# A new order of all work in a block-causal attention with a gated linear unit

## The chip, the core and the metric

The kernel runs on one core of a Trainium2 chip, in one launch. The core has a matrix engine (TensorE, in the profile PE, its weight loads PEld), a vector engine (VectorE, DVE), a scalar engine (ScalarE, ACT), a general engine (GpSimd, POOL) and an engine that here only issues transfers (SyncE, SP). Each runs its own list of instructions in order, and they wait for each other by semaphores. The metric is the device time of one execution in microseconds (us), lower is better. The kernel before takes 177.25 us, the median of 3 runs (176.99 to 177.54).

## The reference

Eight batches of eight heads, 576 positions, head size 64: attention in which a position sees its own block of 64 and all blocks before it. The heads are put side by side (512 columns), a causal convolution with five taps gives a gate, and the gated product goes through a last matrix.

```python
scores = (1.0 / np.sqrt(D)) * np.matmul(q, k.transpose(0, 1, 3, 2))
scores = np.where(block_i >= block_j, scores, -1000000000.0)
attn = np.exp(scores - np.max(scores, axis=-1, keepdims=True))
attn = attn / (np.sum(attn, axis=-1, keepdims=True) + 1e-09)
x = np.matmul(attn, v)                    # heads put side by side: (8, 576, 512)
for k in range(5):
    gate_pre += conv_w[k] * xp[:, k:k + S, :]      # xp: x with 4 rows of zeros ahead
out = ((1 / (1 + np.exp(-gate_pre))) * (x @ w_val)) @ w_out
```

## The kernel before, in words

**The units of work.** A group Q (0 to 15) is half a batch: four heads. Its q and k arrive as one transfer each of 576 KB (`Lq.Q`, `Lk.Q`), are cast to 16 bits (`cq`, `ck`, L156) and turned by 32x32 blocks on DVE (`dq`, `dk`, L202). v arrives in four blocks of 256 KB and a tail of 128 KB for each batch (`Lv.b.j`, `Lvt.b`) and is cast (`cv`, `cvt`). Three pieces of scores for each Q (`s.Q.t`, L233) go to PSUM on PE, and `sl.b` the last key block of a batch. ACT makes the exponentials of a pair of heads p (0 to 31) from them (`e.p.t`, `el`, L242), POOL sets the masked corners to zero (`m.p`, L263 and L264), and `av.p` on PE multiplies with v, whose 65th column of ones gives the sum. DVE divides (`n.p`, a reciprocal at L289 and a product at L290). `xtr.p` turns the result on PE (L298), and `xt.p` copies it to the tile that holds the 512 columns of a batch (L156).

**The second half** runs on n from 0 to 9: n below 8 is the first 512 positions of a batch, 8 and 9 are the last 64 positions of four batches each, gathered by `xe.b`. `cn.n` is the convolution with 80 small matmuls on PE (L328), `th` the tanh form of the gate on ACT (L332), `val.n.x` the product with the value matrix on PE, `gv` gate times value on DVE (L347), `proj` or `o.n.t` the last product on PE, `oc` its copy to a tile (L156) and `st` the store.

**What sets the order.** Nothing is scheduled by a compiler. The text `PLAN` is a list of words. A loop at the end goes through it and issues each word on the engine that stands after the @: A, D, P and S for ACT, DVE, POOL and SP; digits are the PSUM banks for PE, which is then the engine. The order of the words of one engine is the order of its instructions; words of different engines are bound only by data and by buffers. Buffers are rings: six tiles for arriving q and k, eight for v, four for cast q and k, three for turned ones, six for the exponentials, four for the output. PSUM has eight banks, and the plan names each bank by hand: a block of matmuls can start in a bank only when the copy or exponential that reads the work there before is done.

**The start.** While the first transfers are under way, PE multiplies a tile of zeros: `w.512` is one such matmul of 512 columns, `w.256` one of 256. `cw` brings the taps of the convolution (`Lcw`, `cwc`, `cT`, `DG`) into their place; `id`, `fo`, `pk`, `pv`, `pp`, `p4` and `px` fill constants; `Lwv` and `wv` bring the value matrix, `Lwo` and `wo` the last one.

The loop that reads the plan:

```python
for word in PLAN.split():
    name, _, at = word.partition("@")
    f, *a = name.split(".")
    m = [ENG[c] if c in ENG else int(c) for c in at]
    OPS[f](*map(int, a), m[0] if len(m) == 1 else tuple(m))
```

## Time and profile before

| what | value |
|---|---|
| time, median of 3 runs | 177.25 us (176.99 to 177.54) |
| the profiled execution: its time, its span | 176.23 us, 174.4 us |
| PE busy | 161.7 us (93% of the span) |
| ACT busy | 131.5 us (75%) |
| DVE busy | 129.9 us (74%) |
| POOL busy | 69.2 us (40%) |
| moved by DMA | 40.30 MB |
| mean granted PE clock | 0.971 |

The span runs from the first to the last instruction of the profiled execution. The digits of a slice tell the busy share of an engine in tenths, 40 slices of 4.36 us each. The chain of waits is followed back from the last instruction: at each step to what released it. Instructions on PE that read and write the same tiles are merged in the timeline, with their number after an x.

### The profile page before, as it was taken

The numbers are of one execution on the slowest core, as the hardware profiler recorded it, in microseconds if no ns is written. First come the engines' busy times: TensorE is split into PE (matmuls) and PEld (weight loads), VectorE is DVE, ScalarE is ACT, GpSimd is POOL, SyncE is SP. The second block draws the span as 40 slices with busy tenths as digits, with TensorE's granted clock in tenths as the row PEclk, the third lists the DMA queues.
The fourth block names the chain that finished last, engine by engine and source line by source line (L and its number), as shares of the span: only waits on it lengthen the run. The fifth ranks groups of instructions, "written<-read, shape, count | busy, mean of one in ns | idle before, by whom it ended". The sixth has DMA issues, their size and how long they took to land.

```text
span 174.4 us, 6916 instructions
## 1 busy us (share of the span) xinstructions
PE 161.7 (93%) x3013; PEld 94.8 (54%) x3013; DVE 129.9 (74%) x202; ACT 131.5 (75%) x160; POOL 69.2 (40%) x141
## 2 busy tenths in 40 slices
PE   7448999989999999999999999999999999999990
PEld 2123677367445673576366854675437563855640
DVE  1599399998878887879697798779899836741650
ACT  3039999987969899767979799899879698456320
POOL 1284565954595817085505134433603022210000
PEclk9985599999999999999999999999999999999999
DMA  5999997999799699999997596999320005403246
GB/s 176 397 323 296 381 327 195 312 264 301 194 336 271 187 325 334 277 296 319 343 337 242 114 402 198 305 233 357 136 79 2 4 4 194 172 4 120 81 163 241
DMA packets 48216, 40.30 MB, mean 231 GB/s; under 512 B 38453, under 2 KB 38453, under 8 KB 48186
## 3 DMA queue, kind: packets, MB, share of 16 engines
q1 hardware_dynamic: 47898, 39.01, 72.8%
q10 hardware_dynamic: 288, 0.85, 1.4%
q8 instruction: 23, 0.38, 0.9%
q14 instruction: 7, 0.06, 0.1%
HBM read 30.42 MB, written 9.44 MB: 228 GB/s over the span
## 4 chain that ended last, share of the span: by engine, by line
PE 70%; DVE 12%; ACT 7%; issue 5%; DMA 3%; ACTq 0%; DVEq 0%
PE PS L99 65%; ACT pt L242 6%; PE PS L298 5%; DMA qks<-in_q_dram 3%; DVE x L290 3%; DVE qk L156 2%; DVE kT L202 2%; DVE gv L347 2%; DVE qT L202 1%; DVE osb L156 1%; DVE rc L289 1%; ACT osb L156 1%; DVE xt L156 0%; DVE v16t L156 0%; ACT v L156 0%
## 5 line engine op out<-in xcount | busy, mean ns | idle before, releaser
L242 ACT ACTIVATE pt<-PS 128x1024 f16<-128x1024 f32 (+1 forms) x112 | 97.8, 937 | 23.3 <-PE PS L99 20.9
L99 PE MATMUL PS<-qT,kT 32*128 32x64 f16 (+4 forms) x768 | 37.6, 291 | 5.7 <-DVE kT L202 4.5
L99 PEld LDWEIGHTS <-pt 128*128 128x128 f16 x960 | 32.0, 99 | 7.1 <-issue 3.1
L99 PE MATMUL PS<-w_out,gv 128*128 128x512 f16 x144 | 35.3, 380 | 0.1
L347 DVE SCALAR_TENSOR_TENSOR gv<-th,PS 128x512 f16<-128x512 f32 x36 | 24.0, 681 | 14.6 <-ACT th L332 9.3
L156 POOL CAST qk<-qks 128x1152 f16<-128x1152 f32 x22 | 25.3, 1165 | 21.4 <-DVE kT L202 12.3
L99 PE MATMUL PS<-v,pt 128*128 128x65 f16 x896 | 33.0, 195 | 0.9 <-ACT pt L242 0.7
L99 PE MATMUL PS<-xt,w_val 128*128 128x512 f16 x128 | 31.9, 381 | 0.0
L99 PEld LDWEIGHTS <-kT 32*128 32x128 f16 x768 | 16.2, 95 | 28.2 <-issue 16.7
L263 POOL MEMSET pt<- 64x384 f16 x32 | 13.8, 430 | 37.8 <-ACT pt L242 37.1
L290 DVE TENSOR_TENSOR x<-PS,rc 128x640 f16<-128x640 f32 x32 | 26.4, 824 | 1.1
L99 PEld LDWEIGHTS <-w_val 128*128 128x128 f16 x160 | 13.7, 98 | 14.6 <-issue 3.8
L99 PEld LDWEIGHTS <-gv 128*128 128x128 f16 x144 | 12.8, 98 | 14.4 <-issue 0.9
L202 DVE STREAM_TRANSPOSE qT<-qk 128x576 f32<-128x576 f32 x16 | 19.9, 1243 | 0.1
L202 DVE STREAM_TRANSPOSE kT<-qk 128x576 f32<-128x576 f32 x16 | 19.7, 1243 | 0.0
L332 ACT ACTIVATE th<-PS 128x1024 f32<-128x1024 f32 (+1 forms) x20 | 17.7, 947 | 2.2 <-PE PS L99 2.2
L156 DVE COPY osb<-PS 128x512 f32<-128x512 f32 (+1 forms) x20 | 13.4, 671 | 7.3 <-PE PS L99 5.8
L156 ACT COPY osb<-PS 128x512 f32<-128x512 f32 (+1 forms) x17 | 9.7, 583 | 9.0 <-PE PS L99 8.3
L289 DVE RECIPROCAL rc<-PS 128x10 f32<-128x10 f32 x32 | 6.8, 212 | 8.4 <-PE PS L99 5.7
L156 DVE COPY xt<-PS 128x1152 f16<-128x1152 f16 x14 | 10.2, 754 | 3.8 <-PE PS L298 3.7
L156 POOL COPY xtl<-xt 128x272 f16<-128x272 f16 x7 | 3.9, 551 | 22.0 <-DVE xt L156 16.7
L156 POOL CAST v<-vst 128x512 f16<-128x512 f32 x18 | 11.4, 642 | 3.0 <-DMA vst<-in_v_dram 2.4
(45 smaller groups left out, 113.8 us busy)
## 6 DMA issues: line engine op xcount, KB each, us to landing
qks<-in_q_dram SPq DMA_DIRECT2D x16, 576.0 KB, 7.0
qks<-in_k_dram SPq DMA_DIRECT2D x15, 576.0 KB, 7.0
vst<-in_v_dram SPq DMA_DIRECT2D x32, 256.0 KB, 6.4
out_dram<-osb SPq DMA_DIRECT2D x15, 512.0 KB, 4.3
out_dram<-osb SPq DMA_DIRECT2D x5, 256.0 KB, 2.5
vtst<-in_v_dram SPq DMA_DIRECT2D x8, 128.0 KB, 5.4
th<-in_moe_w_val_dram SPq DMA_DIRECT2D x2, 512.0 KB, 8.9
w_st<-in_moe_w_out_dram SPq DMA_DIRECT2D x4, 256.0 KB, 8.7
```

The costliest lines, as they stand in the source:

```text
L99: nc.tensor.matmul(out=out, lhsT=lhsT, rhs=rhs, start=start, stop=stop, skip_group_check=True)
L156: (eng.copy if eng is nc.scalar else eng.tensor_copy)(out=o, in_=i)
L202: m.transpose(out=o.bitcast(fp32)[..., 0], in_=qk16[(2 * Q + i) % NQ16][0:128].bitcast(fp32))
L242: nc.scalar.activation(out=o, in_=i, func=AF.Exp, bias=0.0, scale=0.125)
L263: m.memset(pt[64:128, 0:2, 0:1536].rearrange("p h (t s) -> p h t s", t=3)[:, :, :, 0:64], 0.0)
L289: nc.vector.reciprocal(out=rc, in_=O[:, :, :, 64:65])
L290: nc.vector.tensor_tensor(out=x16[p % NX16][0:128].rearrange("p i h d -> p h i d"), in0=O[:, :, :, 0:64], in1=rc.to_broadcast([128, 2, 5, ...
L298: nc.tensor.transpose(out=f16(bk(m, e))[:, 128 * i:128 * i + 128], in_=x16[(p + e) % NX16][0:128, i, 0:2, 0:64], identity=ident16[0:128, 0 ...
L332: nc.scalar.activation(out=ths[turn(n) % NTH][0:128, 2 * s:2 * s + 2, 0:width(n)], in_=two(slot["cn", n][s])[:, :, 0:width(n)], func=AF.Ta ...
L347: nc.vector.scalar_tensor_tensor(out=gvs[turn(n) % NGV][0:128, e * x:e * x + e, 0:w], in0=ths[turn(n) % NTH][0:128, e * x:e * x + e, 0:w], ...
```

## The change

Only the text `PLAN` is another, and every engine's order with it. The operations are the same, but for the matmuls on zeros: 17 of 512 columns before, now 20 of 512 and 12 of 256. Of the 20, twelve stand in four groups of three between the first scores. Some copies move to another engine: ACT gives up three casts of q, one cast of v, one scaling of the value matrix and the issue of the first k; POOL has six more casts of v, two more of q and one more scaling, one cast of k, one of a v tail and three gathers (`xe`) less; DVE has three gathers, one cast each of q, k and a v tail more, and five casts of v and one output copy less. The plan is two lines longer, so each line of the code below it has a number higher by two. From the diff, the first lines and the place around the seventh convolution (`cn.6`); "..." is left out:

```diff
--- before
+++ after
 PLAN = """
-wz@D pk@D pp.2@P Lq.0@S Lk.0@A Lk.1@S Lq.1@S cq.0@D dq.0@D id Lcw@S ck.0@D dk.0@D ck.1@P dk.1@D
...
+wz@D pk@D Lk.0@S ck.0@D id Lq.0@S Lcw@S pv.1@P cwc@P Lk.1@S dk.0@D w.256@0 w.256@0 w.256@0 w.256@0
...
-o.5.3@0 cv.7.3@D s.15.1@24 xtr.26.2@6 xt.26.2@D oc.5.3@A e.30.1@A xtr.24.2@0 s.14.2@26 xt.24.2@D
-xe.6@P e.31.1@A e.29.2@A m.29@P cn.6@04 o.5.2@6 e.28.2@A val.6.0@7 m.28@P cv.7.0@P th.6.0@A oc.5.2@D
...
+e.28.0@A e.29.0@A o.5.3@0 n.24@D xtr.24.2@4 ck.15@P oc.5.3@A xtr.26.2@2 dk.15@D m.29@P o.5.1@1
+xt.24.2@D oc.5.1@A xt.26.2@D xe.6@D s.15.1@46 cn.6@20 m.28@P e.30.1@A o.5.2@4 oc.5.2@D e.31.1@A
```

**First place: SP and DVE at the start.** The first instructions of SP before (`qks` are the tiles for arriving q and k, numbers 0 and 1 of the first group, 2 and 3 of the second; `vst` those for v). The transfer of the first k stands on ACT there, as ACT's first instruction:

```order
L161 DMA qks_0_72<-in_q_dram 128x1152
L161 DMA qks_3_75<-in_k_dram 128x1152
L161 DMA qks_2_74<-in_q_dram 128x1152
L187 DMA conv_nat_68<-in_moe_conv_w_dram 5x512
L171 DMA vst_0_78<-in_v_dram 128x8x64
L161 DMA qks_4_76<-in_q_dram 128x1152
```

The same place on SP now:

```order
L163 DMA qks_1_73<-in_k_dram 128x1152
L163 DMA qks_0_72<-in_q_dram 128x1152
L189 DMA conv_nat_68<-in_moe_conv_w_dram 5x512
L163 DMA qks_3_75<-in_k_dram 128x1152
L163 DMA qks_2_74<-in_q_dram 128x1152
L173 DMA vst_2_80<-in_v_dram 128x8x64
```

k comes first and alone, and all loads stand in one queue. DVE follows: it casts and turns k before q.

**Second place: DVE from the turned third group to the fourth division** (a division is the pair RECIPROCAL and TENSOR_TENSOR; `DG` is made from the taps). Before:

```order
L202 STREAM_TRANSPOSE qT_2_94<-qk16_0_88 128x18x32
L289 RECIPROCAL rc_1_111<-PS_132 128x10
L290 TENSOR_TENSOR x16_1_114<-PS_132,rc_1_111 128x2x5x64
L202 STREAM_TRANSPOSE kT_2_97<-qk16_1_89 128x18x32
L289 RECIPROCAL rc_0_110<-PS_132 128x10
L290 TENSOR_TENSOR x16_0_113<-PS_132,rc_0_110 128x2x5x64
L399 TENSOR_TENSOR DG_71<-idfold_64,convT_70 128x640
```

Now:

```order
L204 STREAM_TRANSPOSE kT_2_97<-qk16_1_89 128x18x32
L158 CAST qk16_0_88<-qks_4_76 128x1152
L204 STREAM_TRANSPOSE qT_2_94<-qk16_0_88 128x18x32
L401 TENSOR_TENSOR DG_71<-idfold_64,convT_70 128x640
L158 CAST v16t_0_100<-vtst_0_86 64x8x64
L291 RECIPROCAL rc_1_111<-PS_132 128x10
L292 TENSOR_TENSOR x16_1_114<-PS_132,rc_1_111 128x2x5x64
L291 RECIPROCAL rc_0_110<-PS_132 128x10
L292 TENSOR_TENSOR x16_0_113<-PS_132,rc_0_110 128x2x5x64
```

The turn of k of the third group and `DG` stood between the divisions and stand ahead of them now.

**Third place: ACT at the end** (`osb` is the output tile). Before:

```order
L332 ACTIVATE th_0_121<-PS_132 128x1024 x2
L332 ACTIVATE th_1_122<-PS_132 128x2x256 x2
L156 COPY osb_2_128<-PS_132 128x512
L156 COPY osb_3_129<-PS_132 128x512
L156 COPY osb_0_126<-PS_132 128x512
L156 COPY osb_1_127<-PS_132 128x256
L376 DMA out_0_dram<-osb_1_127 128x512
```

Now:

```order
L334 ACTIVATE th_1_122<-PS_132 128x2x256 x2
L334 ACTIVATE th_0_121<-PS_132 128x1024 x2
L158 COPY osb_3_129<-PS_132 128x512 x2
L158 COPY osb_0_126<-PS_132 128x512 x2
L158 COPY osb_1_127<-PS_132 128x512
L378 DMA out_0_dram<-osb_1_127 128x512
```

The last copy was split between ACT and DVE (256 columns each) and is now one copy on ACT; the short pieces (n = 9) stand ahead of those of n = 7.

## The prediction

> **What bounds the kernel now.** I read the page first, for the engine that is full and from when.

> ```profile
> span 174.4 us, 6916 instructions
> PE 161.7 (93%) x3013; PEld 94.8 (54%) x3013; DVE 129.9 (74%) x202; ACT 131.5 (75%) x160; POOL 69.2 (40%) x141
> PE   7448999989999999999999999999999999999990
> PEclk9985599999999999999999999999999999999999
> ```

> PE is full from about the fifth slice on. Before that it is not, and its granted clock falls to half in slices four and five. Next, busy time by stage (PE, PEld, DVE, ACT, POOL in this order):

> ```profile
> 20.00:30.00 10.00, 9.64 (x256) 7.48 (x254) 8.98 (x15) 9.75 (x12) 4.93 (x8) 0.92 0.95 273
> 30.00:40.00 10.00, 9.44 (x165) 5.34 (x164) 9.51 (x15) 9.27 (x12) 7.84 (x16) 1.00 1.09 302
> ```

> There are two regimes. Up to about 44 us ACT and DVE are as full as PE or nearly so, and hand the work to each other. From there PE's tenths are all 9 or more. All real matmuls are the same in both plans, so behind 44 us the new order can win only the small waits left in that stretch. The chain of waits shows the border and one such wait:

> ```profile
> 0.74 5.46 DMA qks<-in_q_dram
> 37.36 0.20 DVE rc L289
> 44.56 9.74 PE PS L99 x164
> 153.33 0.86 PE PS L99 x4
> 170.16 0.03 ACTq L156
> 170.23 0.38 ACT osb L156
> 170.64 0.42 DVE osb L156
> ```

> The 44.56 row opens with `cn.1`, the second convolution. Before it the chain passes DVE again and again (37.36 is the division `n.5`); after it, nearly all is PE up to 170.16. So I work out when `cn.1` starts in the new order, then what changes behind it, then the end.

> **The start: first scores.** Before, the rows are these (DVE casts and turns q, then k; PE then begins):

> ```profile
> 6.23 0.76 DVE L156 CAST qk<-qks 128x1152 f16<-128x1152 f32 x1 [4.84 <-DMA qks<-in_q_dram]
> 7.03 1.26 DVE L202 STREAM_TRANSPOSE qT<-qk 128x576 f32<-128x576 f32 x1
> 8.13 1.28 DVE L156 CAST qk<-qks 128x1152 f16<-128x1152 f32 x1
> 7.65 1.14 POOL L156 CAST qk<-qks 128x1152 f16<-128x1152 f32 x1 [6.19 <-DMA qks<-in_k_dram]
> 10.75 1.42 PE L99 MATMUL PS<-qT,kT 32*128 32x320 f16 x32 [4.51 <-DVE kT L202]
> ```

> q and k share the DMA engines there, issued at the same moment on two queues, so q is usable only at 6.23. Now k has the engines for itself at first. A single load of that size into a quiet queue (the one k load in the stretch 96.5 to 97.5 us) took this:

> ```profile
> L161 SPq DMA_DIRECT2D qks<-in_k_dram x1: 340/340/340, 96.8 to 96.8; - x1
> DMA to landing us min/median/max: 4.3/4.3/4.3
> ```

> Issued at 0.74 as the first was before (the first row of the chain), k lands at 0.74 + 4.3 = 5.1. Bounds: 5.1, and 6.2 if being first brings nothing. I take 5.1, since this row is the same transfer. Then cast 0.76, turn 1.26, cast 0.76, turn 1.26 and four hand-overs of 0.04: 9.3 for the first scores instead of 10.75. The second load has until 7.1 to land, more than q and k together needed before. The taps' matmuls `cw` now stand on PE ahead of the scores; they need only a 10 KB load, the third in the queue, and a POOL cast, which leaves about 1.5 us. The issue of k moves from ACT to SP, so SP issues the second group about 1 us later, behind two loads and the taps; it had landed at 7.7 and 9.1 (POOL's casts begin there) while POOL and DVE need it after 8 and 10. That costs nothing while DVE is still on the first group.

> **The start: exponentials and av.**

> ```profile
> 11.42 7.11 ACT L242 ACTIVATE pt<-PS 128x1024 f16<-128x1024 f32 x9 [8.74 <-PE PS L99]
> 18.70 2.85 ACT L242 ACTIVATE pt<-PS 128x1024 f16<-128x1024 f32 x3 [0.17 <-PE PS L99]
> 21.73 3.77 ACT L242 ACTIVATE pt<-PS 128x1024 f16<-128x1024 f32 x4 [0.17 <-PE PS L99]
> ```

> The same 16 exponentials run first in both plans: 7.11 + 2.85 + 3.77 = 13.7 us. Begun 0.67 behind the first scores, as before (10.75 to 11.42), they run from 10.0 to 23.7 instead of 25.5. PE can feed them: it needs 0.6 to 1 us for a block of scores that feeds two. But the new plan puts `av.1`, the first product with v, behind all scores of two groups, in the bank that `e.3.1` reads. That is the fourth exponential from the end, over at 23.7 - 3 x 0.94 = 20.9 (3.77 for four); before, `av.1` began at 18.7. So the first division `n.1` starts at about 21.85, later than the 20.59 of before:

> ```profile
> 20.59 0.22 DVE L289 RECIPROCAL rc<-PS 128x10 f32<-128x10 f32 x1 [2.90 <-PE PS L99]
> 21.59 1.25 DVE L202 STREAM_TRANSPOSE kT<-qk 128x576 f32<-128x576 f32 x1
> 23.84 0.82 DVE L399 TENSOR_TENSOR DG<-idfold,convT 128x640 f16<-128x640 f16 x1
> ```

> From `n.1` to `n.5` DVE took 37.36 - 20.59 = 16.8 us. In the new order the same instructions stand there without the turn (1.25) and `DG` (0.82), which fill DVE's wait ahead of `n.1`: 14.7, and `n.5` starts at 36.55. So 1.45 us at the first scores become 0.8 us at `n.5`: the work was held by DVE, and DVE got its first division later. From `n.5` to `cn.1` DVE has the same list in both plans (a cast of q or k, three more divisions, two copies), 7.2 us before; the new `cn.1` is at 43.75, **0.8 us earlier**. Bounds: adding the bare DVE durations of these pieces gives about 6.5 us instead of 7.2 (43.05); the cast there can take 1.28 instead of 0.76 when POOL casts at the same time, as the 8.13 row shows beside POOL's at 7.65 (44.3).

> [...]

> The twelve new matmuls on zeros stand between the first scores, where PE waits for ACT to free banks. At 0.22 each with full clock or 0.43 with half they are 2.6 to 5.2 us of PE. The longest group ends at 10.95 + 1.3 = 12.25, the next scores at about 13.2, and ACT is busy with its first four exponentials until 13.7. I take nothing; without this cover it would be all of it.

> **Behind cn.1.** Where the convolution follows the turned result with one block of scores between, PE waits for DVE's copy. At `cn.6`:

> ```profile
> 139.19 0.63 PE L99 MATMUL PS<-qT,kT 32*128 32x448 f16 x16
> 139.76 1.29 PE L298 MATMUL PS<-ident,x 128*128 128x128 f16 x20
> 141.00 0.96 PE L99 MATMUL PS<-qT,kT 32*128 32x320 f16 x16
> 142.00 1.35 PE L99 MATMUL PS<-xt,DG 32*32 32x512 f16 x80
> ```

> A block of scores takes 0.57 on PE when nothing holds it (139.19 to 139.76), yet the convolution starts 1.00 behind the one of 141.00: a wait of 0.43. The new plan puts `o.5.1` between as well, 0.86 (the 153.33 row is such a block), so the wait goes: **-0.4 us**. At `cn.1`, `cn.2` and `cn.4` the pattern stays as it was. The other small waits move about; I set their sum to zero, with -1.5 (most of them gone) and +1.5 us (as many again) as bounds.

> POOL's extra work (six casts of v, two of q, one scaling, less four shorter jobs, some 4 us) lies in its waits:

> ```profile
> POOL pt L263 <- ACT pt L242: 37.1, 17, 7.2
> ```

> It stood idle 37.1 us for exponentials alone. ACT gives up about 5 us, and is not what holds PE behind 44 us. Both count as nothing.

> **The end.** Before, the last matmul ends at 170.16, ACT's half copy at 170.61, DVE's at 171.06, then the last store is issued: 0.9 us. A whole copy on ACT takes 0.6:

> ```profile
> L156 ACT COPY osb<-PS 128x512 f32<-128x512 f32 (+1 forms) x17 | 9.7, 583 | 9.0 <-PE PS L99 8.3
> ```

> The new one ends 0.65 after the last matmul: **-0.2 us**. Bounds -0.3 and +0.5: the last stores now stand closer together.

> **Sum.** -0.8 - 0.4 - 0.2 = -1.4 us of span: 174.4 to 173.0. The profiled execution took 176.23, so it would be 174.8; but it ran 1.0 us below the median of the runs, 177.25, which is my base: **175.85 us**. A difference of 0.3%, 0.5 us, is about what a measurement tells from none.

> **Rivals.** 1, slower: *the clock falls in the hole ahead of the first scores and comes back late.* In the stretches of before (granted clock in the third column from the end):

> ```profile
> 4.50:7.90 3.40, 1.75 (x8) 0.59 (x6) 1.63 (x2) 0.00 (x0) 0.25 (x1) 1.00 1.03 417
> 7.90:11.34 3.44, 0.59 (x20) 0.50 (x24) 3.41 (x4) 0.00 (x0) 3.10 (x7) 1.00 1.12 347
> 14.75:18.17 3.42, 3.13 (x42) 1.20 (x40) 2.94 (x6) 3.42 (x6) 1.82 (x5) 0.50 0.96 330
> 18.17:21.58 3.41, 3.40 (x52) 2.45 (x46) 0.95 (x2) 3.22 (x4) 1.65 (x5) 0.50 1.10 375
> 18.68 1.48 PE L99 MATMUL PS<-v,pt 128*128 128x65 f16 x24
> 21.72 0.90 PE L99 MATMUL PS<-v,pt 128*128 128x65 f16 x24
> ```

> A stretch with PE busy for 1.75 of 3.4 us kept the clock, one with 0.59 lost it; 3.13 at half clock did not bring it back, 3.40 did. The new hole, from about 6.0 to 9.3 with 0.2 of `cw` in it, is shorter than 6.2 to 10.75, and each later stretch has PE busy for half or more, so the clock may hold. If it falls, PE waits for banks between the scores and no stretch is full until the avs come at 20.9. With the clock back at 25 the start loses its gain (177.1, no change). With it back only at 28.4, four avs cost 0.8 more each (24 matmuls in 1.48 against 0.90, scaled to 30) and the turning behind them 0.6: `cn.1` at 46.7 or so, 2.2 late against before; less 0.6 that is 178.8. [...] Chance 0.2 for the late form, 0.08 for the mild one.

> 2, same: *k lands no earlier for being first* (its packets start slowly, or the second load takes half the rate): everything up to `cn.1` is 1.1 us later, worse than before by 0.3; with -0.6 behind, 176.95. The quiet load speaks against it; that all loads stand in one queue speaks for it. 0.08.

> 3, faster still: *most small waits behind 44 us go as well*, -1.5 more: 174.35. For it: each is below 0.5 us and needs only another block of matmuls between. Against: three of the four convolutions keep their pattern. 0.18.

> 4, the change does less than it says at the loads of the last batches: in the new order the last block of v of batch 6 stands on SP behind two stores.

> ```profile
> SPq L378 <- DVE osb L156: 34.8, 5, 19.6
> vst<-in_v_dram SPq DMA_DIRECT2D x32, 256.0 KB, 6.4
> ```

> SP waited up to 19.6 us for an output copy. From that copy (`oc.4.1`) to `av.27` about 13 us of matmuls stand; landing takes 6.4 and the cast 0.6. Some 6 us are spare, so only 0.04, at +1: 176.85.

> **Chances.** Forecast 0.42, with its own range 174.9 to 176.7; faster still 0.18; the mild clock 0.08, k late 0.08 and v late 0.04, all three near 177 and within 0.5 us of no change; slower 0.2. So faster is 0.42 + 0.18 = 0.6, the same 0.2, slower 0.2. The range reaches past case 3, by half of its gain again, to short of case 1's full price: 173.7 to 178.4.

> **What would show it.** First scores at 9.3 and first exponential at 10.0; `av.1` later than 18.7 and `n.1` near 21.9; `cn.1` at 43.75; no wait ahead of `cn.6`; the last store issued 0.65 behind the last matmul. It is wrong if the granted clock is half beyond 22 us, if the first cast starts after 6, or if PE has new gaps of half a microsecond behind `cn.1`.

## The result, and the profile after

The new order is slower: 183.0 us, the median of four runs (182.5 to 184.1), against 177.1 for the kernel before beside it; ratio 1.0338, 95% interval 1.0286 to 1.039. The forecast was 175.85 us, in a range of 173.7 to 178.4. Some executions take longer than the others of the same kernel and are left out of the times; three traces below (`e1`, `e3`, `e7`) are of such executions, and they are read for where PE stands still, not for how long a kernel takes. From the page of the profiled execution, which took 182.5 us:

```profile
span 180.7 us, 6935 instructions
PE 164.0 (91%) x3028; PEld 95.6 (53%) x3028; DVE 131.0 (72%) x202; ACT 127.5 (71%) x155; POOL 72.4 (40%) x145
PE   7498899985999999999996979999999999999990
PEclk9958999999699999999999999999999999999997
```

PE's tenths were all nines from about 44 us before; now there are a 5 and, later, a 6 and a 7, and the granted clock dips a second time. The two spans differ by 6.3 us. Counted on PE's matmuls from `cn.0` on:

| us | before | after | difference |
| --- | --- | --- | --- |
| `cn.0` starts | 28.41 | 28.60 | +0.19 |
| from there to the last matmul: PE without a matmul | 1.43 | 5.88 | +4.45 |
| the same stretch: PE busy | 140.31 | 141.61 | +1.30 |
| from the last matmul to the end of the span | 4.28 | 4.64 | +0.36 |
| span | 174.43 | 180.72 | +6.29 |

So the loss is time in which PE stood still. The timeline of PE has three such holes (idle time and releaser in brackets):

```profile
41.23 0.63 PE L101 MATMUL PS<-qT,kT 32*128 32x448 f16 x15
43.84 0.20 PE L101 MATMUL PS<-qT,kT 32*128 32x64 f16 x1 [1.98 <-issue]
99.24 0.61 PE L101 MATMUL PS<-xtl,w_val 128*128 128x256 f16 x4 [1.75 <-issue]
105.16 0.73 PE L300 MATMUL PS<-ident,x 128*128 128x128 f16 x10 [0.68 <-DVE x L292]
```

They add up to 4.41 us; what is left of the idle time, 1.47, is what it was before. The first hole is odd: fifteen of the sixteen matmuls of `s.4.1` have run, and the last one, which reads and writes the same tiles, starts 2 us later. It can't have waited for data. The chain of waits runs through all three and names nothing for them either, but for 0.1 us of the third, in which the division `n.18` was still under way:

```profile
41.87 1.98 issue
97.49 1.75 issue
104.59 0.57 issue
```

The rest of the loss follows the first hole. Stretches of 3.41 us, of before and then of after (PE busy and its matmuls first, granted clock third from the end):

```profile
42.30:45.71 3.41, 2.96 (x114) 2.18 (x111) 3.02 (x5) 3.19 (x4) 1.21 (x2) 1.00 0.82 166
45.71:49.12 3.41, 3.41 (x37) 1.24 (x22) 2.32 (x3) 3.08 (x4) 3.29 (x6) 1.00 1.02 296
```

```profile
42.30:45.71 3.41, 1.85 (x28) 1.46 (x32) 1.22 (x3) 1.57 (x2) 1.98 (x2) 1.00 1.01 289
45.71:49.12 3.41, 3.41 (x96) 1.70 (x89) 2.70 (x3) 2.41 (x4) 0.60 (x4) 0.50 0.81 177
```

PE was busy for 1.85 of 3.41 us, and in the next stretch the granted clock is 0.50 instead of 1.00 (before: 2.96 of 3.41, and it stays 1.00); there `cn.1` takes 2.29 us to the work behind it instead of the 1.28 that the trace of `e1` shows below, where the clock is full: 1.0 of the 1.30 us.

**What the holes have in common** is the number of instructions between them. The windows from one hole to the next (PE's matmuls in the first x, its weight loads in the second):

```profile
0.00:41.87 41.87, 35.14 (x607) 20.29 (x607) 31.15 (x52) 29.46 (x35) 25.07 (x56) 0.92 0.99 293
41.87:97.50 55.63, 53.46 (x1023) 30.52 (x1023) 46.01 (x67) 44.21 (x55) 22.69 (x42) 0.97 0.94 275
97.50:104.50 7.00, 5.25 (x128) 4.10 (x128) 3.90 (x8) 3.09 (x4) 2.54 (x6) 1.00 0.92 295
```

From the second to the third hole PE has 128 + 128 = 256 instructions, from the first to the second 2046; two more, which these windows don't count, are semaphore waits in PE's own list (at 75.77 and 92.23), and that makes 2048, 8 x 256. And the list of queues has one that carries no data of the kernel:

```profile
q8 instruction: 23, 0.38, 0.8%
w_st<-in_moe_w_out_dram SPq DMA_DIRECT2D x4, 256.0 KB, 10.9
```

It made 23 transfers of 16 KB each, which the page counts with the data on the core's 16 DMA engines, and PE's 3028 matmuls and 3028 weight loads are 23.7 times 256: PE's instructions arrive in blocks of 256. When each block came, by the trace's record of that queue, against PE's work (blocks counted from 0):

| block | PE enters the block ahead | transfer | PE at the border | PE goes on | behind the landing |
| --- | --- | --- | --- | --- | --- |
| after, 5 | 35.98 | 41.27 to 42.45 | 41.67 | 43.84 | 1.39 |
| after, 13 | 92.56 | 96.86 to 97.82 | 97.22 | 99.24 | 1.42 |
| after, 14 | 97.22 (works in it from 99.24) | 102.76 to 103.71 | 104.27 | 105.16 | 1.45 |
| after, 16 | 109.94 | 110.43 to 111.32 | 119.26 | 119.26 | - |
| before, 5 | 36.93 | 40.60 to 41.68 | 42.78 | 43.16 | 1.48 |

A block's transfer starts at the earliest about when PE enters the block before it (in some 20 of the 279 cases counted below it started before that block's first matmul, by 2.0 us at most). With idle DMA engines (block 16) it was there 1.4 us later; between the loads of 36 to 42 us it took 6.5, and PE needs only 4.7 to 9.3 us for 256 instructions in this trace. In the first place the new order has the four loads of the last matrix together on SP, followed by `Lk.6` and `Lq.6`, and they landed 10.9 us after their issue (the second row above; 8.7 before). In the second, SP issued 3.9 MB of loads and stores from 90.7 to 99 us; before, it issued a single v tail from 90.7 to 96.8. The kernel before had one small hole of this kind, at `xtr.6.2`, and I had passed over it:

```profile
43.16 0.55 PE L298 MATMUL PS<-ident,x 128*128 128x128 f16 x7 [0.16 <-issue]
```

### The profile page after: what moved, and what is told of

Read it like the earlier page. It is cut to its first block, busy times and chain, and to the rows that moved or that the text cites. A ratio compares the mean times of both kernels' runs of the same rounds, so it can differ in the third digit from the quotient of the medians.

```text
span 180.7 us, 6935 instructions
## 1 busy us (share of the span) xinstructions
PE 164.0 (91%) x3028; PEld 95.6 (53%) x3028; DVE 131.0 (72%) x202; ACT 127.5 (71%) x155; POOL 72.4 (40%) x145
## 3 DMA queue, kind: packets, MB, share of 16 engines
HBM read 30.42 MB, written 9.44 MB: 221 GB/s over the span
## 4 chain that ended last, share of the span: by engine, by line
PE 69%; DVE 11%; ACT 10%; issue 5%; DMA 2%; DVEq 0%; ACTq 0%
PE PS L101 64%; ACT pt L244 8%; PE PS L300 4%; DVE x L292 3%; DMA qks<-in_k_dram 2%; DVE gv L349 1%; DVE kT L204 1%; DVE xt L158 1%; DVE qT L204 1%; ACT th L334 1%; DVE rc L291 1%; DVE qk L158 1%; ACT osb L158 1%; DVE osb L158 0%; DVE v16t L158 0%
## 5 line engine op out<-in xcount | busy, mean ns | idle before, releaser
L101 PE MATMUL PS<-qT,kT 32*128 32x64 f16 (+4 forms) x768 | 37.0, 289 | 5.3 <-DVE convT L158 2.4
L265 POOL MEMSET pt<- 64x384 f16 x32 | 13.3, 415 | 62.1 <-ACT pt L244 61.7
L101 PEld LDWEIGHTS <-pt 128*128 128x128 f16 x960 | 30.9, 98 | 6.1 <-issue 3.3
L349 DVE SCALAR_TENSOR_TENSOR gv<-th,PS 128x512 f16<-128x512 f32 x36 | 24.1, 682 | 13.3 <-PE PS L101 9.4
L101 PE MATMUL PS<-v,pt 128*128 128x65 f16 x896 | 31.6, 194 | 1.2 <-ACT pt L244 0.8
L158 POOL CAST qk<-qks 128x1152 f16<-128x1152 f32 x23 | 26.9, 1183 | 13.2 <-ACT th L334 6.9
L158 DVE COPY osb<-PS 128x512 f32<-128x512 f32 x19 | 13.0, 686 | 10.2 <-PE PS L101 7.9
L158 POOL CAST v<-vst 128x512 f16<-128x512 f32 x24 | 16.3, 691 | 1.0 <-DMA vst<-in_v_dram 0.4
L158 ACT COPY osb<-PS 128x512 f32<-128x512 f32 x17 | 9.9, 587 | 8.7 <-PE PS L101 8.7
L101 PE MATMUL PS<-xt,DG 32*32 32x512 f16 x640 | 12.4, 408 | 0.6 <-DVE xt L158 0.6
## 6 DMA issues: line engine op xcount, KB each, us to landing
vst<-in_v_dram SPq DMA_DIRECT2D x32, 256.0 KB, 6.6
out_dram<-osb SPq DMA_DIRECT2D x5, 256.0 KB, 2.4
w_st<-in_moe_w_out_dram SPq DMA_DIRECT2D x4, 256.0 KB, 10.9
```

The lines of the kernel that those rows point to most:

```text
L101: nc.tensor.matmul(out=out, lhsT=lhsT, rhs=rhs, start=start, stop=stop, skip_group_check=True)
L158: (eng.copy if eng is nc.scalar else eng.tensor_copy)(out=o, in_=i)
L265: m.memset(pt[64:128, 0:2, 0:1536].rearrange("p h (t s) -> p h t s", t=3)[:, :, :, 0:64], 0.0)
L349: nc.vector.scalar_tensor_tensor(out=gvs[turn(n) % NGV][0:128, e * x:e * x + e, 0:w], in0=ths[turn(n) % NTH][0:128, e * x:e * x + e, 0:w], ...
```

## The experiments

**Theory 1:** PE stands still because its next block of instructions comes late, behind the backlog of transfers; the clock's second fall follows from that. **Theory 2:** the new waits come from the new order of the engines and banks, and the profile only fails to name what ends them. In the diffs of loads and stores stand the words of SP alone, in SP's order.

**e1: the loads of the first place.** Only SP's order changes; every other engine's list is the same.

```diff
-Lvt.2 Lwo.1 Lwo.0 Lwo.2 Lwo.3 Lk.6 Lq.6 Lv.2.1 Lv.2.0 Lv.2.3 Lv.2.2 Lq.7
+Lvt.2 Lv.2.1 Lv.2.0 Lv.2.3 Lv.2.2 Lwo.1 Lwo.0 Lwo.2 Lwo.3 Lk.6 Lq.6 Lq.7
```

> The changed kernel (182.9 us) with only the order on SP between Lvt.2 and Lq.7 altered: the four v blocks of batch 2 stand ahead of the four loads of the last matrix and of Lk.6 and Lq.6; no other engine's order is touched. Theory 1 (PE's next 16 KB of instructions wait behind the backlog of transfers): the instruction block that PE enters at about 41.7 us is there in time, the hole of 2.0 us ahead of xtr.4.2 falls below 0.5, the granted clock does not fall at 45.7 to 49.1 (1.0 us more): 180.0 us. Theory 2 (the new waits come from the order of the engines and banks, and the profile only fails to name what ends them): the hole stays where it is, 182.9 +- 0.5.

Measured: 181.3 us, ratio 1.0237 (1.0174 to 1.03). Block 5 was there 2.5 us after PE entered block 4 (6.5 in the changed kernel), the hole is gone, and the clock stays full there. PE's timeline and the window of the trace of `e1`:

```profile
41.19 0.63 PE L101 MATMUL PS<-qT,kT 32*128 32x448 f16 x16
41.76 1.53 PE L300 MATMUL PS<-ident,x 128*128 128x128 f16 x20
44.13 1.35 PE L101 MATMUL PS<-xt,DG 32*32 32x512 f16 x80 [0.17 <-DVE xt L158]
51.84 1.87 PE L101 MATMUL PS<-w_out,gv 128*128 128x512 f16 x4 [3.00 <-POOL w_out L158]
45.71:49.12 3.41, 3.14 (x20) 1.04 (x19) 2.23 (x4) 3.25 (x5) 0.00 (x0) 1.00 1.08 223
```

`s.5.0` starts at 47.25 instead of 50.73. But my order let the last matrix come late: PE waits 3.0 us for POOL's cast of it ahead of `o.0.0`, and the stand-still at block 13 is still there (1.95). Behind the wait of 3.0 us the clock is half from 50.7 to 57.6. Theory 1 holds for the hole and the clock; the 180 us were not reached, and a wait that I had made myself is part of it. The time alone doesn't settle it: the intervals of the two ratios, 1.0174 to 1.03 and 1.0286 to 1.039, still touch.

**e2 and e3: the second place, and both.**

```diff
-Lk.12 Lq.13 st.2.0 Lk.13 Lq.12 st.1.1 Lv.6.1 st.2.1 Lv.5.0 st.3.0 Lq.15 Lk.15 Lvt.7 Lv.7.3 Lq.14 Lv.6.2 Lv.7.0
+Lk.12 Lq.12 Lv.5.0 Lv.6.1 Lq.13 Lk.13 st.1.1 st.3.0 Lq.15 Lk.15 Lvt.7 st.2.0 Lv.7.3 Lq.14 Lv.6.2 Lv.7.0 st.2.1
```

> The changed kernel with only SP's order from 85 to 120 us altered: Lq.12, Lv.5.0 and Lv.6.1 stand ahead of Lq.13, into the time in which SP waited for Lq.13's buffer, and the stores st.2.0 and st.2.1 behind st.3.0, out of the burst of 91 to 99 us. Theory 1: the holes of 1.9 us at 97.2 and 0.9 us at 104.3 fall below 0.5 each: 182.9 - 2.3 = 180.6 us. Theory 2: no change, 182.9 +- 0.5, the holes stay.

> Both alterations of SP's order. Theory 1: 182.9 - 3.0 - 2.3 = 177.6 us, no hole over 0.5 us ahead of an instruction block. If it comes under 177.1 the rest of the new order is better than the one before, if it stays over 177.6 something else in the new order costs time as well. Theory 2: 182.9 +- 0.5.

Measured: `e2` 182.8 and 184.0 us, ratio 1.0378 (1.0308 to 1.0447), a miss, and its trace is not used here. `e3` took 181.0 us, a single run. In its trace block 5, behind the same loads as in `e1`, was there 3.3 us after its entry, the hole at block 13 has shrunk from 1.75 to 0.41 us and that at block 14 is gone, as theory 1 says. A new wait of 2.98 us stands ahead of `val.5.1`: the stores put behind `st.3.0` made the v tail of batch 6 land at 130.55, and DVE stood behind its cast. So theory 1 is borne out at the blocks, in one trace, and my cure was again paid for elsewhere.

**e4: the old order of the engines with the new order of the loads**, in the kernel before:

```diff
-Lq.4 Lwo.0 Lq.5 Lwo.3 Lvt.2 Lwo.1 Lv.2.0 Lk.5 Lk.6 Lwo.2 Lv.2.2 Lv.2.3 Lq.6 Lv.2.1 Lq.7
+Lq.4 Lq.5 Lk.5 Lvt.2 Lwo.1 Lwo.0 Lwo.2 Lwo.3 Lk.6 Lq.6 Lv.2.1 Lv.2.0 Lv.2.3 Lv.2.2 Lq.7
```

> The kernel before with only SP's order between Lq.4 and Lq.7 altered, to the one of the changed kernel (both q, k, the v tail, the four loads of the last matrix together, Lk.6, Lq.6, then the four v blocks). All engines keep the old order. Theory 1: the instruction block that PE entered at 42.78 with 1.10 us in hand now arrives 0.7 to 2 us later, so that PE stands still for 0.8 to 2.5 us there (0.4 before), and the clock may fall behind it (1 us more): 178 to 180 us. Theory 2: 177.1 +- 0.5, no new hole.

Measured: 177.6 us, ratio 1.0049 (1.0013 to 1.0085). The block came 0.8 us later after its entry than before, and the hole at `xtr.6.2` was 0.86 us. That looked like theory 1 at the lower end, but `e11` below takes its force away.

**e5: the same work, other borders.** Of all runs this tells most: nothing is moved, but 36 more small matmuls stand at the start.

```diff
-w.256@0 (12 times)
+w.64@0 (48 times)
```

> The changed kernel with each of its twelve first matmuls on zeros of 256 columns split into four of 64: the same columns, the same order on every engine, but 36 more matmuls, so that all later work stands 72 instructions further down PE's list and each block of 256 instructions begins 36 matmuls earlier in the work. Theory 1 (instruction blocks come late): the two large holes go to other work. The first, now among the last matmuls of s.4.1, opens inside av.7, from about 40.3 us, and lasts 1.5 to 3 us; the second, now in val.8.1, opens in av.16 or s.9.2; nothing stands still where the holes were. 181 to 185 us. Theory 2 (a wait of that work for data or a bank): the holes stay in s.4.1 and val.8.1, 182.9 +- 0.5.

Measured: 180.2 and 181.7 us, ratio 1.020 (1.0093 to 1.0308). The holes went where theory 1 put them. PE's timeline, and the windows up to and between its first two holes:

```profile
39.50 0.44 PE L101 MATMUL PS<-v,pt 128*128 128x65 f16 x9
40.83 0.63 PE L101 MATMUL PS<-v,pt 128*128 128x65 f16 x15 [0.89 <-issue]
47.85 0.44 PE L101 MATMUL PS<-xt,DG 32*32 32x512 f16 x16 [2.40 <-issue]
0.00:39.95 39.95, 33.52 (x607) 20.19 (x607) 30.20 (x49) 28.91 (x35) 23.75 (x55) 0.96 0.98 294
39.95:46.00 6.05, 4.58 (x128) 3.35 (x128) 4.99 (x8) 4.04 (x5) 3.40 (x4) 1.00 1.05 273
```

The first hole comes again after 607 + 607 instructions, now in the middle of `av.7`: from there to the last matmul of `s.4.1` there are 15 + 6 + 15 = 36 matmuls. The next comes 256 instructions later, in the middle of `cn.1`, where none was; at `s.4.1` and `val.8.1` PE no longer stands still. Theory 2 falls: the work that waited did not wait for anything of its own. The hole of 0.89 was smaller than the 1.5 to 3 I expected, and the one of 2.40 I had not foreseen.

**e6: both cures, closer to the old order.**

```diff
-Lvt.2 Lwo.1 Lwo.0 Lwo.2 Lwo.3 Lk.6 Lq.6 Lv.2.1 Lv.2.0 Lv.2.3 Lv.2.2
+Lvt.2 Lv.2.3 Lwo.1 Lwo.0 Lv.2.1 Lwo.2 Lwo.3 Lk.6 Lq.6 Lv.2.0 Lv.2.2
 ...
-Lk.12 Lq.13 st.2.0 Lk.13 Lq.12 st.1.1 Lv.6.1 st.2.1 Lv.5.0 st.3.0 Lq.15 Lk.15 Lvt.7 Lv.7.3 Lq.14 Lv.6.2 Lv.7.0 Lv.7.1 Lk.14 Lvt.6
+Lk.12 Lq.12 Lv.5.0 Lv.6.1 Lq.13 Lk.13 st.1.1 Lq.14 Lvt.6 Lk.14 st.3.0 Lq.15 Lk.15 Lvt.7 st.2.0 Lv.7.3 Lv.6.2 Lv.7.0 st.2.1 Lv.7.1
```

> The changed kernel with SP's order altered in both places, closer to the old one than in the run with both alterations, which let the last matrix and the v tail of batch 6 come late: two v blocks between the loads of the last matrix, Lq.6 ahead of the other two; Lq.12, Lv.5.0 and Lv.6.1 ahead of Lq.13; Lq.14, Lvt.6 and Lk.14 ahead of st.3.0; st.2.0 and st.2.1 behind it. All other engines keep the changed order. Theory 1: no hole over 0.5 us at a block's beginning, the clock stays full behind 15 us, no wait for the last matrix ahead of o.0.0 nor ahead of val.5.1: 182.9 - 2.0 - 1.0 - 1.75 - 0.7 = 177.4 us, about the time of the kernel before, because the start has brought nothing. Theory 2: 182.9 +- 0.5.

Measured: 180.8 us, ratio 1.0214 (1.0125 to 1.0302), 2.2 us better than the changed kernel (the intervals of the ratios touch) and 3.4 worse than expected. Holes of 0.82 us stay at two blocks (6 and 13, which landed 0.4 us ahead of the need), and there is a new wait. In DVE's and POOL's timelines a cast of v that takes 0.4 us elsewhere takes 2.59 beside two casts on POOL, since k of the last group but one had arrived earlier:

```profile
120.81 2.59 DVE L158 CAST v<-vst 128x512 f16<-128x512 f32 x1
120.33 2.23 POOL L158 CAST qk<-qks 128x1152 f16<-128x1152 f32 x2
```

The copy `xt.22.2` stood behind it, and `s.12.2` and `cn.5` lost 0.66 and 0.43 us more than in the changed kernel.

**e7: the start.** On `e6`, the four groups of three `w.512` between the first scores are taken out, and ten `w.512@2` and two `w.256@2` stand behind `cw@0` instead, in the hole ahead of the scores.

> The kernel with both places of SP's order altered again, and the twelve matmuls on zeros between the first scores taken from there and put behind cw, ten of 512 columns and two of 256, into PE's hole ahead of the first scores (6.5 to 8.9 us). The number of instructions is the same. If the half clock from 8.2 to 15 us and the matmuls on zeros made ACT wait among its first exponentials, as I now hold: the clock stays full past 8.2 us, the 16 first exponentials end at about 23.5 instead of 24.1, n.1 starts at 22.0 instead of 22.7 and cn.1 0.7 us earlier than in the other: 176.7 us where it takes 177.4. If loads and casts set the pace there: within 0.3 us of the other.

Measured: 179.6 and 180.9 us, ratio 1.0163 (1.0059 to 1.0267), not to be told from `e6` in the time; but in the trace the start went the other way. `cn.0` starts at 30.10 instead of 27.91. Stretches of `e6`, then of `e7`:

```profile
8.16:11.57 3.41, 2.45 (x26) 1.18 (x26) 2.43 (x4) 1.63 (x2) 2.83 (x7) 0.58 1.15 324
11.57:14.98 3.41, 2.79 (x44) 0.93 (x44) 3.07 (x7) 3.41 (x6) 1.49 (x5) 0.92 1.05 351
```

```profile
11.57:14.98 3.41, 1.38 (x32) 0.73 (x32) 3.15 (x7) 3.41 (x6) 1.39 (x5) 1.00 1.06 347
14.98:18.39 3.41, 2.44 (x30) 0.91 (x31) 3.21 (x5) 3.20 (x5) 3.22 (x8) 0.68 0.95 257
18.39:21.80 3.41, 3.10 (x34) 1.36 (x34) 0.41 (x1) 3.41 (x4) 1.44 (x4) 0.50 1.01 364
```

The half clock is not avoided but put off, from 8 to 12 us, where PE waits for ACT anyway, to 16 to 26, where the products with v run. The timed runs agree on the clock (mean 0.971 and 0.968, against 0.987 to 0.990 of `e6`). So with the matmuls on zeros between the scores the trace has the clock full from 12.1 us on, without them half from 16 to 26, and for the start my expectation was wrong in its sign; what that is worth in the whole time these runs don't tell.

**e8: the same idea in the kernel before**: nineteen more `w.512` ahead of `s.0.2`.

> The kernel before with 19 more matmuls on zeros of 512 columns ahead of its first scores, in the hole from 6.25 to 10.75 us, where PE waits for q; nothing else is altered (each block of instructions begins 19 matmuls earlier in the work). If the half clock of 11.3 to 21.6 us costs time: the clock stays full, the avs before 22 us take 0.9 instead of 1.5, cn.1 comes up to 0.8 us earlier: 176.2 us against 177.0. If ACT's exponentials and DVE set that stretch: within 0.3 us of the kernel before.

Measured: 176.9 us, ratio 0.9961 (0.9921 to 1.0001): no change that can be told. `cn.0` comes at 28.78 (28.41 before), though the mean clock is 0.986 instead of 0.971. This trace is no clean test: the 34 matmuls on zeros last until 11.45, and the first scores start behind them at 11.39 instead of 10.75. In `e10` below the scores start at 10.81 with the clock full up to 15.0, and `cn.0` comes at 28.47; there the fuller clock brought nothing. The hole of before, behind 13 matmuls of `xtr.4.2` and `xtr.6.2`, moves to 6 matmuls ahead of the end of `s.4.1`: 13 + 6 = 19 earlier, the number added. It grew to 1.05 us, and a second one of 0.51 stands at block 4.

**e9 and e10: borders and loads at once.** In `e9` the changed kernel has its twenty first matmuls on zeros split into 112 of 64 columns, and SP's order of `e6` with `Lq.14 st.2.0 st.2.1` behind `st.1.1`, `Lk.14` left late and `Lvt.6` just ahead of it. In `e10` the kernel before has the nineteen matmuls of `e8`, its first twelve split into 96 of 64 columns, and `o.5.2@6 cn.6@04` for `cn.6@04 o.5.2@6`.

> The changed kernel with both cures at once. SP: as in the run with both places altered, closer to the old order, but Lk.14 stays late (its early arrival had put two POOL casts beside DVE's cast cv.6.0, 2.6 us instead of 0.4) and st.2.0 and st.2.1 follow Lq.14, which waits for its buffer to about 99.9 us. PE: the twenty first matmuls on zeros split into 112 of 64 columns, the same columns, so that each block of instructions begins 92 matmuls earlier in the work; the trace of the changed kernel says that PE then takes 5.7 and 7.3 us over blocks in 36 to 47 us and 6.1, 4.9 and 7.0 over those in 90 to 105, where it took 5.7, 5.9, 4.6, 5.1 and 5.0. Theory 1: no hole over 0.5 us but perhaps one of up to 1 us at the 4.9; 181 - 0.8 - 0.4 - 0.8 - 1.2 = about 177.8 us. Theory 2 (only the order of the engines counts): 182.9 +- 0.5.

> The kernel before with what the runs taught. In the hole ahead of the first scores 19 more matmuls on zeros (the clock stays full; that run lost its gain to holes of 0.5 and 1.05 us at instruction blocks); twelve of them of 512 columns split into 64s, the same columns, so that each block begins 103 matmuls earlier in the work than in the kernel before and PE takes 8.5, 6.4 and 6.6 us over the blocks of 29 to 51 us instead of 7.7, 5.8 and 7.3; and cn.6 behind o.5.2 instead of ahead of it (its wait of 0.43 us goes). Theory 1: no hole at a block, 176.9 - 1.2 - 0.4 = 175.3 to 176 us. Theory 2: only the wait ahead of cn.6 counts: 176.8.

Measured: `e9` 180.1 us, ratio 1.0187 (1.0129 to 1.0245); `e10` 178.7, ratio 1.0106 (1.0049 to 1.0163). In `e9` both crowded places are free of holes over 0.4 us, and the cast of v no longer delays `cn.5`; but other borders now fall badly:

```profile
30.62 0.40 PE L101 MATMUL PS<-xt,DG 32*32 32x512 f16 x5 [0.79 <-issue]
81.55 0.19 PE L101 MATMUL PS<-v16t,pt 128*128 128x65 f16 x1 [2.21 <-issue]
```

In `e10` one block costs 0.95 us, and `o.5.2` in its new place waits 1.11 us for an exponential that reads its bank, more than the 0.43 it was to save.

**e11: one load moved in the kernel before.**

```diff
-Lk.5 Lk.6 Lwo.2 Lv.2.2 Lv.2.3
+Lk.5 Lwo.2 Lv.2.2 Lk.6 Lv.2.3
```

> The kernel before with one load moved on SP: Lk.6 (576 KB) stands behind Lwo.2 and Lv.2.2 instead of ahead of them; all other engines as before. Theory 1: the instruction block that PE entered at 42.78 us, 1.10 us after it had landed, now lands 0.3 to 1.5 us earlier, and the hole of 0.38 us ahead of xtr.6.2 goes; cn.1 at 44.2 instead of 44.56: 177.2 - 0.4 = 176.8 us, hardly to be told from no change in the time, but in the trace. Theory 2: cn.1 stays at 44.56.

Measured: 176.8 us, ratio 0.9992 (0.9955 to 1.0029), and in the trace a miss: block 5 took 6.0 us from its entry, not under 4.7, and the hole was 0.90. But blocks 2 and 4, ahead of the moved load, took 6.5 and 7.0 instead of 5.3 and 5.3. So a block's way varies by more than 1 us between executions of the same loads, and neither this run nor `e4`, with a hole as large from the opposite move, says what one load does. `e1` and `e3` (2.5 and 3.3 us instead of 6.5) are beyond that spread.

**Over all traces.** In the twelve used here 35 blocks landed less than 1.2 us before PE was through with the block ahead, or after it. In 34 of them PE went on 1.04 to 1.63 us behind the landing (median 1.42), whatever work stood there; in one, whose transfer lasted 1.6 us instead of about 1, after 0.8. And over 279 blocks the time from PE's entry to the start of the transfer goes with the backlog, taken as the time until the last load or store issued by then has landed (correlation 0.77; PE's entry is its border with the block ahead, also where it then stands still):

| backlog, us | 0 to 1 | 1 to 3 | 3 to 5 | 5 to 7 | 7 to 9 | 9 to 12 |
| --- | --- | --- | --- | --- | --- | --- |
| blocks | 67 | 29 | 59 | 75 | 42 | 7 |
| median until the transfer starts, us | 0.4 | 1.3 | 1.7 | 2.6 | 3.8 | 4.9 |

Whether the bytes, the packets or the order within a backlog count is not separated by these runs. No version was clearly faster than the kernel before.

## Why the prediction was wrong, by its own steps

**The first scores and the first exponential** came as said, 8.89 and 9.96 us (9.3 and 10.0). From ACT's and DVE's timelines after:

```profile
9.96 4.69 ACT L244 ACTIVATE pt<-PS 128x1024 f16<-128x1024 f32 x5 [7.74 <-PE PS L101]
15.21 8.91 ACT L244 ACTIVATE pt<-PS 128x256 f16<-128x256 f32 x11 [0.56 <-PE PS L101]
22.70 0.22 DVE L291 RECIPROCAL rc<-PS 128x10 f32<-128x10 f32 x1 [3.79 <-PE PS L101]
```

The exponentials did not run without a pause: ACT waited 0.56 us, and `n.1` came at 22.70, not 21.85. By the rows below the matmuls on zeros, priced at nothing, made that pause. The second group of three ran at half clock (granted 0.50 from 8.2 to 15.0 us), and the scores behind it are those that ACT waited for. PE's timeline, and the chain of waits, which passes PE there:

```profile
13.38 1.46 PE L101 MATMUL PS<-wz 128*128 128x512 f16 x3
14.78 0.59 PE L101 MATMUL PS<-qT,kT 32*128 32x64 f16 x18
11.04 4.15 PE PS L101 x37
```

In `e6`, whose clock is full again from 12.1 us instead of 15.0, the sixteen exponentials run without a pause from 9.94 to 23.43 and `n.1` starts at 22.01. So in these two traces this price goes with when the clock comes back; without the groups (`e7`) the trace has `cn.0` 2.2 us later. Nor is the time from `av.1` to `n.1` what the sum has: 1.19 us (21.51 to 22.70), not 0.95. From `n.1` to `n.5` it was 14.73 us, as worked out (14.7).

`cn.1` starts at 44.08, 44.13 and 43.86 in the three traces of the new order without a hole over 0.3 us ahead of it (`e6`, `e1`, `e3`): 0.4 to 0.7 us earlier than before instead of 0.8, inside the bounds. But before's 44.56 contains a small hole of its own (block 5 in the table). The order of before without one there, `e10`, has 44.30, so that like for like the start brought only 0.2 to 0.4 us. This term was right in mechanism and mis-sized by about half a us; `cn.0` alone differs by 0.9 us between traces of the same order on every engine but SP (27.72 in `e3`, 28.60 after), so it can't be told more closely.

**cn.6**: right. It starts 0.57 behind the block of scores ahead of it, as long as these take:

```profile
147.07 0.63 PE L101 MATMUL PS<-qT,kT 32*128 32x448 f16 x16
147.64 1.50 PE L101 MATMUL PS<-xt,DG 32*32 32x512 f16 x80
```

**"The other small waits move about; I set their sum to zero", with -1.5 and +1.5 us as bounds: the step that failed.** For waits on data and banks it was right (1.47 us against 1.43). But the bounds counted only those. The three holes of 4.41 us and the half clock behind the first, 1.0, together 5.4 of the 6.3 us of span, are a cost that had no term: I followed the moved loads to their own users and never asked what else uses the DMA engines. The sign that I gave for being wrong, new gaps of half a microsecond behind `cn.1`, showed it; the first stands just ahead of `cn.1`. That the holes are the blocks' is shown (`e5`, the 34 landings); that the order of the loads makes them late is shown for the first place (`e1`, `e3`) and only likely for the second (`e3` in one trace, `e2` not in the time).

**The end**: the last store was issued 0.65 us behind the last matmul, as said,

```profile
176.12 0.58 ACT L158 COPY osb<-PS 128x512 f32<-128x512 f32 x1 [0.65 <-PE PS L101]
176.74 0.37 ACTq L378 DMA_DIRECT2D out_dram<-osb  x1
```

but the span ended 4.0 us after that issue instead of 3.3. The term was +0.36, near its upper bound of +0.5, not -0.2.

**The rivals.** The first scores at 8.89 leave no room for a late k. The clock did not come back late at the start (full from 15 us on); it fell a second time for a reason that was not on the list. The late v block of batch 6 did not happen.

**Without the blocks** the new order would still not have been faster: the three holes and the half clock taken from the 6.29 us of the first table, +0.9 us are left in that execution. The run with both cures says the same: the span of `e6`, 178.7, less its four holes at blocks (0.25, 0.82, 0.82 and 0.36) and the waits behind the cast beside POOL (1.1), is 175.3, 0.9 us over before's 174.4. These are subtractions within single traces, not runs. The end has 0.4 of that; the rest is spread over many words, and I have not located it.

## What to carry to other kernels

Where an engine runs thousands of unrolled instructions near its limit, as PE does here with 6056, take its instruction blocks for one more load with a due time: here 256 instructions, sent when the block ahead was entered or later (but for some 20 of 279), and used 1.42 us after landing when they came late (median of 34); look for holes in the middle of uniform work, count instructions between them, and hold the times against the instruction queue. Before loads are gathered or moved forward, ask what the backlog delays besides their own users, and treat a saving by borders as fragile: 36 added matmuls moved the holes in `e5`, 19 in `e8`. Matmuls on zeros in the longest hole gained no time here (`e7`, `e8`); in the trace of `e7` they were missed: the clock was half from 16 to 26 us, where the products with v run, and in that of `e6` full from 12.1.
